# Laying out a small replicated identity matrix on GpSimd instead of VectorE, in a gated scan followed by a soft mixture of experts

## The chip, the core and the metric

The kernel runs on one core of one Trainium2 chip. The core has five engines that each work through their own list of instructions: TensorE (PE in the profile, with PEld for its weight loads), VectorE (DVE), ScalarE (ACT), GpSimd (POOL) and SyncE (SP), which issues the DMA transfers between HBM and the on-chip memory SBUF. TensorE writes its results to a second on-chip memory, PSUM. The engines wait for one another through semaphores. The metric is the device time of one execution in microseconds; a lower time is better.

## The reference

Two layers are computed one after the other. The first is a gated linear recurrence over 5056 time steps, for 4 sequences of 256 channels:

```python
sig_r, sig_i = sigmoid(r_gate), sigmoid(i_gate)
a_t = exp(8 * sig_r * log(sigmoid(a_param)))
x_gated = sqrt(max(1 - a_t * a_t, 1e-6)) * sig_i * x
h = a_t[:, t] * h + x_gated[:, t]          # for each t; y[:, t] = h
```

The second is a soft mixture of 8 experts with 4 slots each, over all 4 x 5056 = 20224 tokens of y (called x below):

```python
logits = x @ phi                                   # 20224 x 32
d = exp(logits - logits.max(0)); d /= d.sum(0) + 1e-9
slot_input = d.T @ x                               # 32 slots x 256
h = maximum(slot_input[e] @ w1[e], 0); slot_out[e] = h @ w2[e]   # each expert e
c = exp(logits - logits.max(1)); c /= c.sum(1) + 1e-9
out = c @ slot_out                                 # 20224 x 256
```

## The kernel before

The 20224 tokens are cut into 40 blocks of up to 512 and 22 units: unit 0 holds one block, units 1 to 18 hold two, the last three hold one. Each unit goes through a fixed set of steps, and a step is a small function that issues one or a few instructions. The names below are those of the order lists.

- `Dr`, `Di`, `Dx` (SP) load the r gate, the i gate and x of a unit.
- `SR`, `SI` (ACT, lines 810 and 828) take the tanh of the gates; `EX` (ACT, 884) makes a_t; `SQ` (mostly POOL, 869) squares it; `RT` (ACT, 900) takes the root of 1 - a_t². ACT works in phases, because tanh and exp on one side and the root on the other need different function tables (ACT_TABLE_LOAD). The roots of three or four units are taken together.
- `U` multiplies the i gate by x for one block, on POOL (850) or, for blocks 2, 8 and a few others, on DVE (848).
- `TU` (PE, 917) transposes a unit's half of U into PSUM; `ST` (DVE, 940) multiplies it by the root; `SC` (DVE, 960) runs the recurrence. In `ST1.0` the first number is the unit and the second the half of the channels.
- `TY` (PE, 983) transposes the result back, `YC` (DVE 999 or ACT 997) copies it from PSUM, `LG` (PE, 1042) makes the logits, `LE` (DVE, 1056) copies them with their running maximum, `TE` (PE, 1066 and 1070) transposes them, `ES` (ACT, 1079) takes the exponentials, `AC` (PE, 1095) sums the slots' inputs.
- Once all units are done, the slots' inputs are merged, the experts run (PE, 1357 and 1409), and for each unit the result is made (PE, 1559), copied (1574, 1576) and stored (SP, 1587).

All data live in one SBUF tensor `all_s` of 49 slots. A planner with a model of durations hands out slots and fixes, for each engine, where TensorE gets filler multiplications of `half_id` (line 1234), which compute nothing that is used. The order of the steps on each engine is written out by hand in the table `ORDER`, one list an engine, and the planner follows it.

The change touches `const` and `const2`. `const` (POOL, lines 692 to 701) builds the 128 x 128 identity `ident`, a bf16 copy `half_id`, its negative `minus`, and a few columns of ones. `const2` (DVE, lines 705 to 709) writes a column `eps` and `R`: 4 x 4 copies of a 32 x 32 identity, which serves as a matrix for sums over groups of partitions. `R` is read for the first time by step `W` (line 1302), after the last scan, and `eps` by the steps `RB` (line 1496), later still. Each of the four copies writes 32 partitions by 128 elements, reading a 32 x 32 piece of `ident` four times over. Before, `const2` stands in the list of DVE between `SC0.1` and `ST1.1`.

Of the kernel before, what the change touches and what calls it, by code (L numbers as in the profile page):

```python
# [11 lines left out]
AF = mybir.ActivationFunctionType  # L12
# [4 lines left out]
J = 4  # L17
# [68 lines left out]
SHIFT = {}  # L86
ORDER = {
    "DVE": (
# [13 lines left out]
    ),  # L102
    "ACT": (
# [27 lines left out]
    ),  # L131
    "POOL": (
# [5 lines left out]
    ),  # L138
# [91 lines left out]
class Planner:  # L230
# [15 lines left out]
    def add(self, eng, name, dur, deps=(), prio=0.0, emit=None, lat=None, alloc=(), uses=(), **kw):  # L246
        eng = eng if isinstance(eng, tuple) else (eng,)
        if lat is None:
            lat = {"PE": 0.25, "ACT": 0.13, "DVE": 0.13, "POOL": 0.12, "SP": 0.05}[eng[0]]
        if eng[0] == "PE":  # L250
            dur *= PEX
        t = Task(eng, name, dur, lat, deps, prio + KOFF.get(re.match("[A-Za-z]+", name)[0], 0.0) + EARLY.get(name, 0.0), emit, alloc, uses, **kw)
        self.tasks.append(t)
        for b in [*alloc, *uses]:
            b.users += 1
        return t
# [308 lines left out]
def kernel(  # L565
# [11 lines left out]
    nc = tc.nc if tc is not None else None  # L577
    B, S, D = x.shape
    E, _, FF = w1.shape
    NS = phi.shape[1]  # L580
# [33 lines left out]
    if tc is not None:  # L614
# [18 lines left out]
        ident = sb.tile([P, P], F32, name="ident")  # L633
# [6 lines left out]
        R = sb.tile([P, J, NS], F32, name="R")  # L640
        ones = sb.tile([1, 1], F32, name="ones")
        eps_sb = sb.tile([P, 1], F32, name="eps")
# [7 lines left out]
    def t(buf):  # L650
        if buf.tag == "s":
            a, n = buf.slot[0], len(buf.slot)
            return all_s[:, a : a + n, :] if n > 1 else all_s[:, a, :]
        if buf.tag == "one" and buf.slot[0] >= len(T["one"]):
            single_banks()
        v = T[buf.tag][buf.slot[0]]
        return v[:, 0, :] if buf.tag == "pair" and buf.tags != ("pair",) else v

    add = planner.add
# [43 lines left out]
    t_const = add("POOL", "const", 0.75, prio=-100, emit=e_const)  # L703

    def e_const2():
        nc.vector.memset(eps_sb, 1e-9)
        for j in range(J):
            v = slice(32 * j, 32 * j + NS)
            nc.vector.tensor_copy(out=R[v], in_=ident[v, v].rearrange("p (o s) -> p o s", o=1).broadcast_to([NS, J, NS]))  # L709

    t_const2 = add("DVE", "const2", 0.9, deps=[t_const], prio=-50, emit=e_const2)


    chunk_of = {}
# [496 lines left out]
    for nm, q in order:  # L1211
        p = q if nm == "r" else unit[q][0]
# [50 lines left out]
    def last_y(pl, tag):  # L1263
# [4 lines left out]
               emit=lambda: nc.gpsimd.memset(t(sT)[:, : E * H * NS], 0.0))  # L1268
# [82 lines left out]
    for e in range(E):  # L1351
# [11 lines left out]
        if not e:  # L1363
# [6 lines left out]
                       prio=-30 + e, emit=e_l1,  # L1370
# [33 lines left out]
    for e in range(E):  # L1404
# [10 lines left out]
        if e == E - 1:  # L1415
            half = [slice(0, P), slice(P, D)]
            l2s = [add("PE", "L2.7", 0.44, deps=[hr[e // EB], wts[("w2", e)][1]], gate=begun(l2_prev),
                       prio=-30 + e + 5.2, emit=lambda f=e_l2: f(cs=half[0]), uses=[wts[("w2", e)][0], hz, so], shape="C")]
# [4 lines left out]
                      prio=-30 + e + 5.2, emit=e_l2, alloc=[] if e else [so],  # L1423
# [4 lines left out]
    def e_rc(v):  # L1428
        if planner.cur.eng_used == "ACT":
            nc.scalar.copy(out=t(soRb)[:, v], in_=t(sr)[:, v])  # L1430
        else:
            nc.vector.tensor_copy(out=t(soRb)[:, v], in_=t(sr)[:, v])

    t_sw = []
    for k, (n_so, n_rs, n_sw) in enumerate((("SO", "RS", "SW"), ("SV", "RV", "SX"))):
        v = half[k]
# [5 lines left out]
                        emit=lambda v=v: e_rc(v), alt={"ACT": 0.21}))  # L1442
# [76 lines left out]
    for i, g in enumerate(corder):  # L1519
# [25 lines left out]
        for p in gunits[g]:  # L1545
# [40 lines left out]
            def e_od(og=og, a0=quads(p0)[0] * QT, c=per_part(p) * (2 if both else 1)):  # L1586
# [4 lines left out]
                deps=group_ev if both else ev, prio=pr + 4, emit=e_od, uses=[og], kind="out", lat=LATO)  # L1591
# [82 lines left out]
```

## Time and profile before

| what | value |
|---|---|
| time, median of 3 runs | 291.35 us (291.05 to 292.14) |
| time of the profiled execution | 290.35 us |
| its span, first to last instruction | 288.6 us |
| mean granted TensorE clock | 0.968 |
| PE busy / DVE busy / ACT busy / POOL busy | 254.1 / 234.2 / 237.1 / 187.0 us |
| HBM read and written | 78.94 MB and 20.71 MB |

The profile records one execution. A busy time is the sum over the span, so it doesn't say where an engine waits. Views used below are the timeline (each row: start, duration, engine, line, operation, output <- inputs, shapes, count, and in brackets the idle time before and what ended it), the chain of work that ended last, and busy time by stretches.

### The profile page before, as it was taken

To read this page: it belongs to the slowest core of one execution; us is meant where nothing else is said; L and a number is where in the kernel's file an instruction comes from. 1 tells how busy PE (TensorE), PEld (TensorE's weight loads), DVE (VectorE), ACT (ScalarE), POOL (GpSimd) and SP (SyncE) were. 2 spreads that over 40 slices of the span, in tenths; PEclk is the share of its full clock that TensorE was granted. 3 is DMA by queue.
4 is the path that set the end of the run, shared out by engine and by line. 5 is a ranking of instruction groups with operands and counts; after the bars stand their busy time and mean duration, and the time that the engine had idled before them with its cause. 6 is when DMAs were issued, how large, how long until landed. Compare 5 with 4: busy or idle time off the path is not lost.

```text
span 288.6 us, 5895 instructions
## 1 busy us (share of the span) xinstructions
PE 254.1 (88%) x2428; PEld 169.4 (59%) x2428; DVE 234.2 (81%) x277; ACT 237.1 (82%) x237; POOL 187.0 (65%) x120
## 2 busy tenths in 40 slices
PE   6999949889999799899899998999999999999800
PEld 2455634665777468568466766666766566656500
DVE  0025999999999999999899999999985579879720
ACT  6999999809999999999999999999980357877500
POOL 2379989399698999998997999996300321222000
PEclk9999986999999999999999999999999999999975
DMA  7999999999966989989999999987770029999995
GB/s 234 412 427 417 420 422 425 417 420 420 408 260 246 420 334 394 417 304 378 340 357 413 419 414 353 400 309 230 250 320 2 2 108 407 417 437 403 429 426 253
DMA packets 14956, 100.02 MB, mean 347 GB/s; under 512 B 1745, under 2 KB 2002, under 8 KB 4306
## 3 DMA queue, kind: packets, MB, share of 16 engines
q1 hardware_dynamic: 14928, 99.65, 85.9%
q8 instruction: 19, 0.31, 0.4%
q14 instruction: 7, 0.06, 0.1%
q10 hardware_dynamic: 2, 0.00, 0.0%
HBM read 78.94 MB, written 20.71 MB: 345 GB/s over the span
## 4 chain that ended last, share of the span: by engine, by line
PE 36%; DVE 25%; ACT 21%; issue 8%; POOL 5%; DMA 1%; DVEq 0%; ACTq 0%; POOLq 0%
DVE all_s L960 11%; PE one L1234 9%; DVE pair L940 7%; PE bank L1559 6%; ACT all_s L884 5%; ACT all_s L900 4%; ACT all_s L828 4%; POOL all_s L869 3%; ACT all_s L810 3%; PE bank L1234 3%; ACT yn L997 3%; PE pair L917 3%; PE bank L1357 2%; PE bank L1409 2%; DVE R L709 2%
## 5 line engine op out<-in xcount | busy, mean ns | idle before, releaser
L960 DVE TENSOR_TENSOR_SCAN all_s<-all_s,pair 128x1024 f32<-128x1024 f32 (+8 forms) x50 | 93.2, 1880 | 0.6
L850 POOL TENSOR_TENSOR all_s<-all_s 128x1024 f32<-128x1024 f32 (+1 forms) x37 | 88.2, 2404 | 5.1 <-ACT all_s L828 3.2
L869 POOL TENSOR_TENSOR all_s<-all_s 128x1024 f32<-128x1024 f32 (+2 forms) x42 | 71.8, 1735 | 22.1 <-ACT all_s L884 15.8
L917 PE MATMUL pair<-ident,all_s 128*128 128x128 f32 x480 | 60.2, 278 | 7.9 <-DVE all_s L960 6.7
L917 PEld LDWEIGHTS pair<-ident,all_s 128*128 128x128 f32 x480 | 53.8, 142 | 16.6 <-DVE all_s L960 7.4
L940 DVE SCALAR_TENSOR_TENSOR pair<-all_s,pair 128x1024 f32<-128x1024 f32 (+1 forms) x38 | 44.7, 1187 | 2.9 <-ACT all_s L900 2.6
L983 PE MATMUL pair<-ident,all_s 128*128 128x128 f32 x316 | 41.5, 277 | 2.5 <-ACT yn L997 1.7
L884 ACT ACTIVATE all_s<-all_s,ca 128x2048 f32<-128x2048 f32 (+3 forms) x28 | 43.4, 1587 | 0.1
L1234 PE MATMUL one<-half_id 128*128 128x512 bf16 x157 | 41.0, 406 | 0.0
L983 PEld LDWEIGHTS pair<-ident,all_s 128*128 128x128 f32 x316 | 34.4, 140 | 11.2 <-ACT yn L997 4.5
L1506 POOL TENSOR_TENSOR all_s<-all_s,rs_all 128x512 f32<-128x512 f32 (+3 forms) x12 | 10.7, 896 | 43.4 <-DVE rs_all L1503 43.4
L1234 PEld LDWEIGHTS <-half_id 128*128 128x128 bf16 x222 | 21.9, 102 | 28.4 <-issue 10.5
L828 ACT ACTIVATE all_s<-all_s 128x2048 f32<-128x2048 f32 (+2 forms) x22 | 37.9, 1730 | 0.0
L810 ACT ACTIVATE all_s<-all_s 128x2048 f32<-128x2048 f32 (+2 forms) x22 | 37.4, 1729 | 0.6 <-DMA all_s<-in_r_gate_dram 0.6
L900 ACT ACTIVATE all_s<-all_s 128x2048 f32<-128x2048 f32 (+2 forms) x22 | 37.1, 1733 | 0.1
L1095 PE MATMUL one<-yn,eS 128*32 128x257 f32 x312 | 22.5, 386 | 2.6 <-ACT eS L1079 1.8
L1574 ACT COPY all_s<-bank 128x512 f32<-128x512 f32 (+1 forms) x37 | 18.8, 551 | 7.2 <-PE bank L1559 5.9
L1042 PE MATMUL one<-all_s,phi_sb 128*32 128x256 f32 (+1 forms) x344 | 23.6, 368 | 0.8 <-DVE all_s L960 0.7
L997 ACT COPY yn<-pair 128x1024 f32<-128x1024 f32 (+1 forms) x24 | 23.2, 987 | 0.0
L1576 DVE COPY all_s<-bank 128x512 f32<-128x512 f32 (+1 forms) x28 | 17.7, 653 | 4.4 <-PE bank L1559 3.2
L999 DVE COPY yn<-pair 128x1024 f32<-128x1024 f32 x16 | 19.3, 1208 | 0.0
L1559 PE MATMUL bank<-all_s,eS 32*128 32x256 f32 x200 | 18.6, 395 | 0.0
(110 smaller groups left out, 302.3 us busy)
## 6 DMA issues: line engine op xcount, KB each, us to landing
all_s<-in_r_gate_dram SPq DMA_DIRECT2D x18, 1024.0 KB, 10.7
all_s<-in_i_gate_dram SPq DMA_DIRECT2D x18, 1024.0 KB, 10.8
all_s<-in_x_dram SPq DMA_DIRECT2D x18, 1024.0 KB, 9.9
all_s<-in_moe_w_dram SPq DMA_DIRECT2D x16, 1024.0 KB, 7.9
out_dram<-all_s SPq DMA_DIRECT2D x5, 2048.0 KB, 9.6
out_dram<-all_s SPq DMA_DIRECT2D x8, 1024.0 KB, 6.5
all_s<-in_i_gate_dram SPq DMA_DIRECT2D x3, 512.0 KB, 8.1
all_s<-in_x_dram SPq DMA_DIRECT2D x3, 512.0 KB, 10.0
```

The lines of the kernel that those rows point to most:

```text
L810: nc.scalar.activation(v, v, AF.Tanh, scale=0.5)
L828: nc.scalar.activation(v, v, AF.Tanh, scale=0.5)
L850: eng.tensor_tensor(out=o, in0=a, in1=b, op=ALU.mult)
L869: eng.tensor_tensor(out=t(Nb[(p, h)])[:, :c], in0=v, in1=v, op=ALU.mult)
L884: nc.scalar.activation(v, v, AF.Exp, scale=ca[:, h : h + 1], bias=ca[:, h : h + 1])
L900: nc.scalar.activation(v, v, AF.Sqrt, bias=f, scale=-f)
L917: nc.tensor.matmul(t(up)[:, i, m * P : (m + 1) * P], raw(nm, q)[:, m * D + h * P : m * D + (h + 1) * P], ident, is_transpose=True, start=( ...
L940: nc.vector.scalar_tensor_tensor(v, w, 1e-3 if gate_of(quads(p)[0]) == "S" else 0.5e-3, u, op0=ALU.max, op1=ALU.mult)
L960: nc.vector.tensor_tensor_scan(dst, dst, flat()[:, s0:s1], init, op0=ALU.mult, op1=ALU.add)
L983: nc.tensor.transpose(out=flat()[:, b * D + h * P : b * D + (h + 1) * P], in_=t(A[p])[:, h, i * QT + (b0 + b) * P : i * QT + (b0 + b + 1) ...
L1234: nc.tensor.matmul(t(b)[:, 0, :] if b.tag == "pair" else t(b), half_id, half_id.rearrange("p (o c) -> p o c", o=1).broadcast_to([P, J, P]) ...
L1559: nc.tensor.matmul(t(op)[:, k * D : (k + 1) * D], t(hT)[r, (k0 + k) * P : (k0 + k + 1) * P], t(soRb)[r, :D], start=True, stop=True)
```

## The change

The step `const2` moves from DVE to POOL, with all of its five instructions, and from its place behind the first scan to the very beginning, directly behind `const`. The planner's estimate of it goes from 0.9 to 1.3 us. In the table, `const2` leaves the DVE list and enters the POOL list; the other lists keep their names and their order.

```diff
     "DVE": (
-        "CA SQ2.1 U2 ST0.0 ST0.1 SC0.0 SC0.1 const2 ST1.1 SC1.1 ST1.0 SC1.0 ST2.0 SC2.0 ST2.1 SC2.1 ST3.0 YC1.0 SC3.0 "
+        "CA SQ2.1 U2 ST0.0 ST0.1 SC0.0 SC0.1 ST1.1 SC1.1 ST1.0 SC1.0 ST2.0 SC2.0 ST2.1 SC2.1 ST3.0 YC1.0 SC3.0 YC3.0 U8 "
...
     "POOL": (
-        "const SQ3.1 SQ3.0 SQ0.1 SQ0.0 U0 SQ1.0 SQ1.1 U1 SQ2.0 U3 P14 U4 U6 U5 SQ5.1 SQ5.0 SQ4.0 SQ4.1 U7 SQ6.1 SQ6.0 "
+        "const const2 SQ3.1 SQ3.0 SQ0.1 SQ0.0 U0 SQ1.0 SQ1.1 U1 SQ2.0 U3 P14 U4 U6 U5 SQ5.1 SQ5.0 SQ4.0 SQ4.1 U7 SQ6.1 "
...
     def e_const2():
-        nc.vector.memset(eps_sb, 1e-9)
+        nc.gpsimd.memset(eps_sb, 1e-9)
         for j in range(J):
             v = slice(32 * j, 32 * j + NS)
-            nc.vector.tensor_copy(out=R[v], in_=ident[v, v].rearrange("p (o s) -> p o s", o=1).broadcast_to([NS, J, NS]))
+            nc.gpsimd.tensor_copy(out=R[v], in_=ident[v, v].rearrange("p (o s) -> p o s", o=1).broadcast_to([NS, J, NS]))
 
-    t_const2 = add("DVE", "const2", 0.9, deps=[t_const], prio=-50, emit=e_const2)
+    t_const2 = add("POOL", "const2", 1.3, deps=[t_const], prio=-50, emit=e_const2)
```

In the built program DVE had these instructions around the place (`SC0.1`, then `const2`, then `ST1.1`, `SC1.1`, `ST1.0`); line numbers are those of the kernel before.

```order
L960 SCALAR_TENSOR_TENSOR all_s<-all_s,pair_74 128x512
L706 MEMSET eps 128x1
L709 COPY R<-ident 32x128 x4
L940 SCALAR_TENSOR_TENSOR pair_75<-all_s,pair_75 128x1024
L960 SCALAR_TENSOR_TENSOR all_s<-all_s,pair_75 128x1024
L940 SCALAR_TENSOR_TENSOR pair_73<-all_s,pair_73 128x1024
```

After the change `ST1.1` stands directly behind `SC0.1`. (Its line numbers are higher by one, since the POOL list takes one more line.)

```order
L961 SCALAR_TENSOR_TENSOR all_s<-all_s,pair_73 128x512
L961 SCALAR_TENSOR_TENSOR all_s<-all_s,pair_74 128x512
L941 SCALAR_TENSOR_TENSOR pair_75<-all_s,pair_75 128x1024
L961 SCALAR_TENSOR_TENSOR all_s<-all_s,pair_75 128x1024
L941 SCALAR_TENSOR_TENSOR pair_73<-all_s,pair_73 128x1024
```

On POOL the end of `const` and the first squares stood like this before the change.

```order
L697 TENSOR_SCALAR minus<-ident 128x128
L699 MEMSET yn_65 128x4
L700 MEMSET ones 1x1
L701 MEMSET one_sb 128x1
L869 TENSOR_TENSOR all_s<-all_s 128x1024 x2
L869 TENSOR_TENSOR all_s<-all_s 128x512 x2
```

After it, the five instructions stand between the last of `const` and the first square.

```order
L701 MEMSET ones 1x1
L702 MEMSET one_sb 128x1
L707 MEMSET eps 128x1
L710 COPY R<-ident 32x128 x4
L870 TENSOR_TENSOR all_s<-all_s 128x1024 x2
L870 TENSOR_TENSOR all_s<-all_s 128x512 x2
```

The lists of ACT and SP hold the same instructions in the same order, and every tile in `all_s` keeps its slot. On PE one filler multiplication is left out: three instead of four stand between `TU2.0` and `TU2.1`.

## Rows read from the trace of the kernel before

**Rows 1.** The chain that ended last, 29 to 41 us: start, us, what

```profile
30.21 1.32 PE pair L917 x12
...
33.03 1.08 DVE R L709
...
38.93 1.24 DVE pair L940
```

**Rows 2.** Timeline of DVE, 25 to 67 us

```profile
28.83 2.33 DVE L960 TENSOR_TENSOR_SCAN all_s<-all_s,pair 128x512 f32<-128x512 f32 x2
31.08 1.94 DVE L709 COPY R<-ident 32x128 f32<-32x128 f32 x1
...
33.03 5.87 DVE L709 COPY R<-ident 32x128 f32<-32x128 f32 x3
...
52.98 1.21 DVE L940 SCALAR_TENSOR_TENSOR pair<-all_s,pair 128x1024 f32<-128x1024 f32 x1
...
58.59 2.83 DVE L848 SCALAR_TENSOR_TENSOR all_s<-all_s 128x1024 f32<-128x1024 f32 x1
```

**Rows 3.** Timeline of POOL, 25 to 67 us

```profile
30.57 2.37 POOL L850 TENSOR_TENSOR all_s<-all_s 128x1024 f32<-128x1024 f32 x1
32.92 1.12 POOL L838 TENSOR_SCALAR all_s<-all_s,one_sb 128x1024 f32<-128x1024 f32 x1
34.12 7.02 POOL L850 TENSOR_TENSOR all_s<-all_s 128x1024 f32<-128x1024 f32 x3
...
56.59 3.75 POOL L869 TENSOR_TENSOR all_s<-all_s 128x1024 f32<-128x1024 f32 x2 [4.64 <-issue]
60.30 3.33 POOL L850 TENSOR_TENSOR all_s<-all_s 128x1024 f32<-128x1024 f32 x1
```

**Rows 4.** Timeline of ACT, 25 to 75 us

```profile
26.54 6.46 ACT L900 ACTIVATE all_s<-all_s 128x1024 f32<-128x1024 f32 x4
...
49.24 4.07 ACT L884 ACTIVATE all_s<-all_s,ca 128x2048 f32<-128x2048 f32 x2
...
64.42 0.49 ACT L1079 ACTIVATE eS<-one 128x384 f32<-128x384 f32 x1 [7.51 <-PE one L1070]
...
66.23 7.31 ACT L900 ACTIVATE all_s<-all_s 128x2048 f32<-128x2048 f32 x4
```

**Rows 5.** Three stretches: PE, PEld, DVE, ACT, POOL busy; clock, DMA, GB/s

```profile
57.00:64.40 7.40, 5.38 (x46) 4.01 (x43) 7.40 (x8) 0.00 (x0) 7.40 (x4) 1.00 1.01 421
64.50:209.00 144.50, 135.81 (x1329) 97.46 (x1327) 141.69 (x123) 144.13 (x118) 128.92 (x71) 1.00 0.90 353
209.00:288.60 79.60, 63.50 (x779) 39.62 (x777) 51.29 (x125) 39.35 (x85) 11.23 (x13) 0.93 0.70 292
```

**Rows 6.** Timeline of the first 13 us, POOL and DVE

```profile
1.37 0.29 POOL L696 CAST half_id<-ident 128x128 bf16<-128x128 f32 x1
1.63 0.53 POOL L697 TENSOR_SCALAR minus<-ident 128x128 f32<-128x128 f32 x1
...
12.06 1.89 POOL L869 TENSOR_TENSOR all_s<-all_s 128x1024 f32<-128x1024 f32 x1 [9.67 <-ACT all_s L884]
...
4.33 0.17 DVE L1146 TENSOR_SCALAR ca<-ca 128x2 f32<-128x2 f32 x1 [4.33 <-ACT ca L1130]
```

**Rows 7.** Timeline of PE, 30 to 50 us

```profile
36.58 1.47 PE L917 MATMUL pair<-ident,all_s 128*128 128x128 f32 x12
...
42.60 2.82 PE L917 MATMUL pair<-ident,all_s 128*128 128x128 f32 x12 [3.68 <-DVE all_s L960]
45.22 3.74 PE L1234 MATMUL one<-half_id 128*128 128x512 bf16 x9
```

**Rows 8.** The load of x for unit 8, and the POOL multiplications that read it

```profile
L748 SPq DMA_DIRECT2D all_s<-in_x_dram x1: 327/327/327, 61.2 to 61.2; - x1
...
DMA to landing us min/median/max: 12.4/12.4/12.4
...
82.25 4.71 POOL L850 TENSOR_TENSOR all_s<-all_s 128x1024 f32<-128x1024 f32 x2 [0.67 <-ACT all_s L828]
```

33 rows, old and new, of the table ORDER are left out of this document.

## The prediction

> **What bounds the kernel now.** I began with the chain that ended last. Around 31 to 39 us it runs through the copies that write `R`, the step that the change moves: the transposes `TU1.1` end at 31.53, then comes `R`, and only at 38.93 the next real work of DVE, `ST1.1` [rows 1]. So the moved step isn't small work hidden somewhere; at this place DVE is what the chain waits for.
>
> The timeline of DVE says how long [rows 2]. Its two scans of unit 0 end at 28.83 + 2.33 = 31.16. The copies begin at 31.08 and the last ends at 33.03 + 5.87 = 38.90. Four copies of 32 x 128 elements thus hold DVE for 7.8 us, while a scan over 128 x 512 takes 1.2. The reader is to compare the ends of the copies with the ends of POOL's instructions [rows 3]: POOL ends one at 30.57 + 2.37 = 32.94, the next at 34.04, and three of 2.34 each at about 36.5, 38.8 and 41.1. The copies end at 33.02, at 34.11 [rows 1] and the last at 38.90, each just behind the end of a POOL instruction. A copy waits for POOL's running instruction and then needs less than 0.1 us.
>
> The timeline of ACT tells whether anybody needs those 7.8 us [rows 4]. ACT idles for 7.51 us before `ES0` at 64.42, so it was free at 56.91; `ES0` waits for `TE0` of PE, which waits for `LE0` of DVE. From there on ACT is the bound: in the 144.5 us from 64.5 to 209 it is busy for 144.13 [rows 5]. DVE is busy for 141.69 there, POOL for 128.92, and the DMA engines at 0.90. The rest, 209 to 288.6, begins when the last scans are through.
>
> So the idle time of ACT is the one large hole in an otherwise closed sequence, about as long as what DVE loses to the copies.
>
> **The change, part by part.**
>
> Removed from DVE: from 31.16, where DVE would be free, to 38.93, where `ST1.1` starts: 7.77 us. The memset of `eps` lies inside.
>
> What is late next: `ST1.1` also needs `TU1.1`, which ends at 31.53 [rows 1], and the third of the four roots. The four end at 26.54 + 6.46 = 33.00 and the large ones take about 1.8 each [rows 4], so the third ends at 31.2. `ST1.1` starts at about 31.55, and 0.39 of the 7.77 goes. That leaves 7.38.
>
> Added to POOL: one memset and four copies, behind `const` at about 2.4 us. The trace has no such copy on POOL. Nearest is the cast of the identity, 128 x 128 with one input, 0.29 us; the bound from above is `minus` at 0.53, from below nothing [rows 6]. I take 0.29, since it too is a copy of the same length along the partition: 4 x 0.29 + 0.1 = 1.3 us, so POOL ends at 3.7. The cover is POOL's idle time of 9.67 us up to 12.06 [rows 6]; without it the 1.3 us would lie on POOL's squares. The next DVE instructions, which make `ca`, start at 4.33, behind that end. Cost 0.
>
> PE has one filler less between `TU2.0` and `TU2.1`: about 0.2 us, where PE waited 3.68 us before [rows 7]. Worth nothing by itself.
>
> Is DVE then held elsewhere? From 38.93 to 52.98 there are four pairs of a multiplication and a scan, 3.51 each [rows 1, 2]. `ST2.0` would start at 31.55 + 7.03 = 38.6; its transposes `TU2.0` end at 36.58 + 1.47 = 38.05, whatever DVE does [rows 7]. Half a microsecond of room. `ST3.0` would start at 45.6. Its transposes stand on PE behind three fillers, `TU2.1`, nine fillers and the logits of unit 2. Four fillers took from 38.05 to 38.92 (42.60 less the wait of 3.68), 0.22 each; the nine took 3.74, or 0.42 each, behind the long wait, where the twelve transposes also took 2.82 instead of 1.47 [rows 7]. By 0.22 the nine end at 42.2, just when unit 2's scan ends, and the logits (some 0.6) and sixteen transposes (2.0) at 44.8: in time. By 0.42 it is 46.5, and 0.9 us is lost. I take 0, because the wait that went ahead of the slow pace is gone, and keep 0.9 for the range.
>
> `U8`, on DVE with two inputs in SBUF, took 2.83 us while POOL was at work; a multiplication of the same shape with one input in PSUM takes 1.21 [rows 2]. It moves to 51.2. POOL has a hole there, from 51.95 (56.59 less 4.64) [rows 3]; `U8` ends by 53.2 instead of 54.0, another 0 to 0.9 us. I count none of it, since the next term caps the gain.
>
> `ES0` comes at 64.42 - 7.38 = 57.04, with ACT free at 56.91. ACT's hole shrinks to 0.1, and its whole closed block moves forward by 7.4. More than 7.51 isn't to be had here.
>
> Can the others follow? POOL: the fourth root of the second group starts at about 66.23 + 3 x 1.8 = 71.7, after the change at 64.3, and needs the squares of unit 7 [rows 4]. POOL waited 4.64 us before the squares of unit 6; they need the exponentials that end at 49.24 + 4.07 = 53.31. From 53.4: two squares 3.75, one multiplication 2.37 to 3.33, two squares 3.75, so 63.3 to 64.2 [rows 3, 4]. It just fits. The loads: DMA is full from 57 to 64.4 (1.01, 421 GB/s) [rows 5], so these can't come sooner. The tightest that I found is x of unit 8, issued at 61.2 and landed 12.4 later, at 73.6; it is used at 82.25, then at 74.9 [rows 8]. It fits by 1.3. Later, DMA has a tenth to spare and the issues move with the slots that come free.
>
> Sum: -7.77 + 0.39 + 0 + 0 = -7.4 us. The profiled execution goes from 290.35 (span 288.6 and 1.75 around it) to 283.0. The median of the runs stands 1.0 higher, and I carry the difference over: 291.35 - 7.4 = **284.0**.
>
> **A rule to weigh.** The rows show copies that end 0.1 us behind POOL's instructions, and pairs of `ST` and `SC` that keep 3.51 us throughout. The Trainium skill, SBUF — State Buffer, section "SBUF: two separate sides", says that VectorE and GpSimd share a pair of ports as an exclusive lock, which a VectorE instruction takes in a two-port mode or with two SBUF inputs, and that the loser blocks for the other's whole instruction. The trace agrees in the copies (7.8 us for four). It speaks against the change in one respect: copies on GpSimd could hold the lock against the instructions that make `ca`. By the rule with 0.29 each the lock is free at 3.7 and the sum stays -7.4.
>
> **The rivals.**
> - *POOL doesn't follow.* The profile names nothing that ended POOL's wait of 4.64 us. If the squares of unit 6 can't start before 56.59, those of unit 7 end where they did, about 67.4, instead of 64.3 when ACT wants them: 3.1 lost, 291.35 - 4.3 = 287.1. For it: the wait is unexplained and POOL's fit is within 0.1 to 1. Against: it is more likely a wait for a slot that PE and DVE free, which moves too. A load tighter than the one I found, or slow fillers (284.9), lie in the same region.
> - *The wait only finds another victim.* DVE's next instructions would wait for POOL's in the place of the copies: 291.3. For: POOL works without a break from 30.57 to 41.1 [rows 3]. Against: two scans ran in 2.33, and the pairs took 3.51 beside a busy POOL [rows 2].
> - *Slower.* GpSimd could be very slow at reading a 32-element piece four times over; no row shows it. The squares at 12.06 would then be late, and `U0` and the first scans behind them. This decides from an end at 12.06 + 7.4 = 19.5, that is over 4.2 us a copy; at 5 us, POOL ends at 22.5 and the time is 291.35 - 7.4 + 10.4 = 294.4. Against: 0.29 to 0.53 for 128 partitions.
>
> **How the numbers follow.** Full gain 70% (283.0 to 284.9), part of it 18% (284.9 to 288), the other victim 8% (290 to 291.8), slower 4%. The likeliest gives 284.0. Dropping the last two cases and the upper end of the second, the range is 282.9 to 287.2; its lower end allows for 1 us from a shorter `U8` and from the spread of the runs (1.1). Under 0.5% (1.5 us) this kernel's measurement can't tell a change from none. Faster by more: 70 + 18 and a little of the third, 89%. Same: 7%. Slower: 4%.
>
> **What would show it.** `ST1.1` at about 31.6; no copy of `R` on DVE; five POOL instructions that end before 4.3; ACT's idle time before `ES0` under 1 us; the squares of unit 6 at 53 to 54; ACT still without a gap until about 201; the last span about 281. I am wrong if DVE's next instructions stretch, if ACT's hole comes back in front of a root or a tanh, or if loads end a wait of ACT or POOL after 57 us.

## The result and the profile after

| | before | after |
|---|---|---|
| median of the runs shown together | 291.06 us (289.14 to 292.14, 6 runs) | 283.38 us (282.77 to 283.72, 6 runs) |
| profiled execution | 290.35 us | 283.55 us |
| its span | 288.6 us | 281.8 us |
| DVE busy / ACT busy | 234.2 / 237.1 us | 225.7 / 237.0 us |

The ratio is 0.9736, with an interval of 0.9703 to 0.9768: 7.7 us less by the medians, where 7.4 were forecast. The kernel before spreads by 3 us from run to run (289.14 to 292.14), and beside e9 to e12 below the same two kernels took 289.22 and 282.9 us, 6.3 apart. So the size of the gain is known only to about a microsecond.

The timelines of the changed kernel answer to those of before. First POOL in its first 13 us, for [rows 6]:

```profile
2.31 0.09 POOL L707 MEMSET eps<- 128x1 f32 x1
2.34 1.27 POOL L710 COPY R<-ident 32x128 f32<-32x128 f32 x4
```

The four copies take 1.27 us together and end at 3.61, before DVE's next work on `ca` at 3.87. Then DVE from 25 to 67 us, for [rows 2]:

```profile
29.55 2.32 DVE L961 TENSOR_TENSOR_SCAN all_s<-all_s,pair 128x512 f32<-128x512 f32 x2
32.11 1.23 DVE L941 SCALAR_TENSOR_TENSOR pair<-all_s,pair 128x1024 f32<-128x1024 f32 x1 [0.23 <-PE pair L918]
...
51.77 1.99 DVE L849 SCALAR_TENSOR_TENSOR all_s<-all_s 128x1024 f32<-128x1024 f32 x1
...
54.82 0.54 DVE L1057 TENSOR_SCALAR_CACHE_REDUCE all_s<-one 128x384 f32<-128x384 f32 x1
```

`ST1.1` follows the scans after 0.23 us, in which DVE waits for the transposes. `U8` (line 849) takes 1.99 us, where it took 2.83. ACT in the same time, for [rows 4]:

```profile
27.25 6.47 ACT L901 ACTIVATE all_s<-all_s 128x1024 f32<-128x1024 f32 x4
...
53.95 3.71 ACT L829 ACTIVATE all_s<-all_s 128x2048 f32<-128x2048 f32 x2
57.56 0.47 ACT L1080 ACTIVATE eS<-one 128x384 f32<-128x384 f32 x1
...
59.34 7.31 ACT L901 ACTIVATE all_s<-all_s 128x2048 f32<-128x2048 f32 x4
```

The row of `ES0` has no bracket any more: the hole of 7.51 us is gone, and ACT goes from one tanh to `ES0` without a stop. POOL, for [rows 3]:

```profile
31.29 2.38 POOL L851 TENSOR_TENSOR all_s<-all_s 128x1024 f32<-128x1024 f32 x1
...
50.30 2.38 POOL L851 TENSOR_TENSOR all_s<-all_s 128x1024 f32<-128x1024 f32 x1
54.12 3.75 POOL L870 TENSOR_TENSOR all_s<-all_s 128x1024 f32<-128x1024 f32 x2 [1.44 <-ACT all_s L885]
57.83 2.39 POOL L851 TENSOR_TENSOR all_s<-all_s 128x1024 f32<-128x1024 f32 x1
60.17 3.75 POOL L870 TENSOR_TENSOR all_s<-all_s 128x1024 f32<-128x1024 f32 x2
```

POOL waited 4.64 us before the squares of unit 6; now it waits 1.44, and what ends the wait is named: the exponentials of ACT. PE, for [rows 7]:

```profile
37.06 1.47 PE L918 MATMUL pair<-ident,all_s 128*128 128x128 f32 x12
38.37 0.81 PE L1235 MATMUL one<-half_id 128*128 128x512 bf16 x3
39.02 1.47 PE L918 MATMUL pair<-ident,all_s 128*128 128x128 f32 x12
40.33 2.11 PE L1235 MATMUL one<-half_id 128*128 128x512 bf16 x9
```

The second twelve transposes take 1.47 us instead of 2.82, and the nine fillers 2.11 instead of 3.74. Busy time by stretches, for [rows 5]; the last two are the stretches behind `ES0` and behind the last scans:

```profile
49.60:57.00 7.40, 6.21 (x53) 4.38 (x53) 7.40 (x8) 7.40 (x5) 5.96 (x4) 1.00 1.01 422
57.00:201.60 144.60, 135.21 (x1323) 96.73 (x1322) 141.03 (x122) 144.24 (x117) 132.83 (x73) 1.00 0.94 374
201.60:281.80 80.20, 63.98 (x783) 40.11 (x781) 51.75 (x126) 39.83 (x87) 11.23 (x13) 0.93 0.71 292
```

Ahead of the second stretch ACT is now busy for 7.40 of 7.40 us, where it did nothing for as long. Behind it the time is the same, though POOL and the loads are a little busier there (132.83 against 128.92 us, 374 against 353 GB/s). From `ES0` to the end of the span there are 288.6 - 64.42 = 224.2 us before and 281.8 - 57.56 = 224.2 after, and the four roots that started at 66.23 [rows 4] start at 59.34, 6.9 earlier. The whole gain lies ahead of `ES0`.

The chain that ended last says the same. Before, it went through `R` on DVE [rows 1]; after, in 25 to 66 us, it is on ACT once `U2` on DVE is through:

```profile
24.57 2.69 DVE all_s L849
...
27.25 6.47 ACT all_s L901 x4
...
57.66 0.37 ACT eS L1080
...
59.34 7.31 ACT all_s L901 x4
```

One difference between the two profiled executions isn't the change. In the one after, the third load of the r gate ended a longer wait of ACT at the start:

```profile
9.50 1.91 ACT L811 ACTIVATE all_s<-all_s 128x2048 f32<-128x2048 f32 x1 [1.75 <-DMA all_s<-in_r_gate_dram]
```

Before, that row began at 8.79, behind 0.57 us. All that ACT does from there on is 0.71 us late, up to the first roots (27.25 against 26.54 [rows 4]). The kernel of before with one tanh left out (e8 below) has this wait too, at 1.69 us, and over all of the traces below it lies between 0.91 and 1.99, whatever the kernel. So it varies from execution to execution, and the profiled pair shows -7.5 + 0.7 = -6.8 us. The medians show -7.7, which is 0.2 more than the hole held and within the spread of the runs.

### The profile page after: what moved, and what is told of

The parts are those of the page before. It is cut to its first block, busy times and chain, and to the rows that moved or that the text cites. A ratio compares the mean times of both kernels' runs of the same rounds, so it can differ in the third digit from the quotient of the medians.

```text
span 281.8 us, 5894 instructions
## 1 busy us (share of the span) xinstructions
PE 251.6 (89%) x2427; PEld 167.7 (60%) x2427; DVE 225.7 (80%) x272; ACT 237.0 (84%) x237; POOL 187.0 (66%) x125
## 4 chain that ended last, share of the span: by engine, by line
ACT 41%; PE 26%; DVE 8%; issue 8%; DMA 6%; POOL 4%; SPq 2%; DVEq 0%; ACTq 0%
ACT all_s L885 10%; ACT all_s L901 8%; ACT all_s L811 8%; ACT all_s L829 7%; DMA all_s<-in_x_dram 6%; PE bank L1560 6%; DVE all_s L961 4%; PE bank L1235 3%; ACT yn L998 3%; PE bank L1358 3%; PE bank L1410 3%; DVE pair L941 2%; POOL all_s L870 2%; PE pair L918 2%; POOL all_s L851 2%
## 5 line engine op out<-in xcount | busy, mean ns | idle before, releaser
L851 POOL TENSOR_TENSOR all_s<-all_s 128x1024 f32<-128x1024 f32 (+1 forms) x37 | 87.0, 2371 | 1.6 <-DMA all_s<-in_x_dram 1.2
L918 PE MATMUL pair<-ident,all_s 128*128 128x128 f32 x480 | 58.9, 275 | 4.5 <-DVE all_s L961 3.0
L918 PEld LDWEIGHTS pair<-ident,all_s 128*128 128x128 f32 x480 | 52.7, 140 | 13.2 <-issue 5.7
L984 PE MATMUL pair<-ident,all_s 128*128 128x128 f32 x316 | 41.5, 277 | 2.6 <-ACT yn L998 1.7
L984 PEld LDWEIGHTS pair<-ident,all_s 128*128 128x128 f32 x316 | 34.4, 140 | 11.2 <-ACT yn L998 4.5
L1235 PE MATMUL one<-half_id 128*128 128x512 bf16 x156 | 39.6, 397 | 0.0
```

The lines of the kernel that those rows point to most:

```text
L851: eng.tensor_tensor(out=o, in0=a, in1=b, op=ALU.mult)
L918: nc.tensor.matmul(t(up)[:, i, m * P : (m + 1) * P], raw(nm, q)[:, m * D + h * P : m * D + (h + 1) * P], ident, is_transpose=True, start=( ...
L984: nc.tensor.transpose(out=flat()[:, b * D + h * P : b * D + (h + 1) * P], in_=t(A[p])[:, h, i * QT + (b0 + b) * P : i * QT + (b0 + b + 1) ...
L1235: nc.tensor.matmul(t(b)[:, 0, :] if b.tag == "pair" else t(b), half_id, half_id.rearrange("p (o c) -> p o c", o=1).broadcast_to([P, J, P]) ...
```

## The experiments

Theory: the copies were dear because each waited for the GpSimd instruction that was running, and they stood on the path to `ES0`, the one hole of ACT. Any place or form without that wait is worth the same, up to the point where ACT has no hole left. The rivals: it is GpSimd's speed or the early place that matters; it is the mere occupation of DVE; or ACT isn't what sets the pace afterwards. All ratios are to the kernel before on the same chip, which took 289.88 us beside e1 to e4, 290.39 beside e5 to e8 and 289.22 beside e9 to e12. The changed kernel itself ran beside e9 to e12 only, with a ratio of 0.979 (e11).

**e1: on DVE, but at the beginning.** The table of DVE, against the kernel before:

```diff
-        "CA SQ2.1 U2 ST0.0 ST0.1 SC0.0 SC0.1 const2 ST1.1 ...
+        "CA const2 SQ2.1 U2 ST0.0 ST0.1 SC0.0 SC0.1 ST1.1 ...
```

> The step stays on VectorE and moves alone, to directly behind the two instructions that make ca, at about 4.4 us, when GpSimd is idle. My theory (the four copies are short and only wait for GpSimd's running instructions): each copy takes at most 0.15 us there, and the time is that of the changed kernel, 283.4 us within 0.7. Rival (the copies are slow on VectorE by themselves, 1.9 us each): four copies of about 1.9 us in the rows, still hidden ahead of 19 us, so the time would be 283.4 too and the rows decide. Rival (the engine is what counts, not the place): about 291.

Measured: 283.46 us, ratio 0.9789 (0.9743 to 0.9835). In the timeline of DVE:

```profile
4.56 0.21 DVE L709 COPY R<-ident 32x128 f32<-32x128 f32 x1
...
4.78 0.68 DVE L709 COPY R<-ident 32x128 f32<-32x128 f32 x3
```

DVE needs 0.22 us a copy when POOL is idle, more than the 0.15 expected, against 1.95 at the old place. The ratio is that of e11, so GpSimd itself isn't needed for the gain.

**e2: on POOL, but in the middle.** The table of POOL, against the changed kernel:

```diff
-        "const const2 SQ3.1 SQ3.0 SQ0.1 SQ0.0 U0 SQ1.0 SQ1.1 U1 SQ2.0 U3 P14 U4 ...
+        "const SQ3.1 SQ3.0 SQ0.1 SQ0.0 U0 SQ1.0 SQ1.1 U1 SQ2.0 U3 const2 P14 U4 ...
```

> The step goes to GpSimd, but to the place in GpSimd's list that runs at about 33 us, between U3 and P14, where it ran on VectorE before. My theory: the copies take about 0.3 us each, 1.3 in all; U4 and the transposes behind it come 1.3 late, the second multiplication of VectorE 0.9 late, of which 0.8 is room ahead of ES0; 283.4 to 284.2 us. Rival (GpSimd is as tight as ScalarE there, all 1.3 us count): 284.7. Rival (only leaving GpSimd's busy stretch helps): near 291.

Measured: 283.03 us, ratio 0.977 (0.9722 to 0.9817). The timeline of POOL:

```profile
33.42 1.27 POOL L710 COPY R<-ident 32x128 f32<-32x128 f32 x4
34.79 1.12 POOL L839 TENSOR_SCALAR all_s<-all_s,one_sb 128x1024 f32<-128x1024 f32 x1
35.99 7.02 POOL L851 TENSOR_TENSOR all_s<-all_s 128x1024 f32<-128x1024 f32 x3
42.97 3.75 POOL L870 TENSOR_TENSOR all_s<-all_s 128x1024 f32<-128x1024 f32 x2
```

In the middle of POOL's other work, with DVE busy too, the copies take their 1.27 us, as at the start. What they delay is taken up where POOL had 0.9 us of idle time before the squares at 42.97, which now follow at once. The early place isn't needed either.

**e3: the old place on DVE, in another form.** A reduction over one element writes the same numbers:

```diff
-            nc.vector.tensor_copy(out=R[v], in_=ident[v, v].rearrange("p (o s) -> p o s", o=1).broadcast_to([NS, J, NS]))
+            nc.vector.tensor_reduce(out=R[v], in_=ident[v, v].rearrange("p (o s u) -> p o s u", o=1, u=1).broadcast_to([NS, J, NS, 1]), axis=AX.X, op=ALU.max)
```

> VectorE, the old place, the old sizes; only the operation differs: a maximum over one element (a reduction) in place of a copy. My theory (the wait belongs to the form of the instruction, which wants what GpSimd holds): if a reduction doesn't want it, four of at most 0.3 us, ST1.1 about 0.9 us later than in the changed kernel, of which 0.8 is room: 283.4 to 284.2 us. Rival (any VectorE instruction that reads and writes SBUF waits for GpSimd at this place): four of about 1.9 us and 291 us.

Measured: 283.31 us, ratio 0.978 (0.9731 to 0.9829). The timelines of POOL and of DVE at the place:

```profile
31.42 2.38 POOL L850 TENSOR_TENSOR all_s<-all_s 128x1024 f32<-128x1024 f32 x1
33.78 1.13 POOL L838 TENSOR_SCALAR all_s<-all_s,one_sb 128x1024 f32<-128x1024 f32 x1
...
31.93 0.27 DVE L709 TENSOR_REDUCE R<-ident 32x128 f32<-32x128 f32 x1
...
32.22 0.86 DVE L709 TENSOR_REDUCE R<-ident 32x128 f32<-32x128 f32 x3
33.11 1.23 DVE L940 SCALAR_TENSOR_TENSOR pair<-all_s,pair 128x1024 f32<-128x1024 f32 x1
```

One POOL instruction runs from 31.42 to 33.80, and the four reductions run right through it, 0.28 us each. Same engine, same place, same bytes: 7.8 us as copies, 1.2 as reductions. Alone, the four copies take 0.9 us (e1), so 6.9 of the 7.8 us at the old place were the wait for POOL, and the wait comes with the form of the instruction: the copy has it, the reduction hasn't. The remaining 1.2 us of DVE cost nothing that the runs can tell. The Trainium skill, SBUF — State Buffer, section "SBUF: two separate sides", ties the wait to a two-port mode or to two inputs in SBUF. By the Trainium skill, VectorE: DVE Perf Modes, section "The perf-mode tier table (the rule you actually need)", a reduction has only the plain mode. The trace agrees, with 0.28 against 1.95 us beside a busy POOL.

**e4: on DVE, late.** `const2` stands in DVE's table between `MX` and `AE10`, shortly before `R` is first read:

```diff
-        "... RR3 AE9 MX AE10 W AE11 ...
+        "... RR3 AE9 MX const2 AE10 W AE11 ...
```

> VectorE, but late: between MX and AE10, after the last scan, where GpSimd is idle and VectorE waited 0.47 us. My theory: four copies of about 0.1 us, inside that wait, 283.4 us within 0.7. Rival (slow on VectorE by themselves): four of 1.9 us on the path to the experts, 283.4 + 7.3 = 290.7.

Measured: 283.47 us, ratio 0.9785 (0.9734 to 0.9836), with 0.21 us for the first copy at 205.84 and 0.68 for the other three. The place costs nothing once POOL has little to do.

**e5 and e6: one or three copies stay on DVE at the old place**, the others are made by POOL at the beginning. Against the changed kernel, for e5 (3 in the place of 1 for e6):

```diff
-        for j in range(J):
+        for j in range(1, J):
...
+    def e_const3():
+        for j in range(1):
+            v = slice(32 * j, 32 * j + NS)
+            nc.vector.tensor_copy(out=R[v], in_=ident[v, v].rearrange("p (o s) -> p o s", o=1).broadcast_to([NS, J, NS]))
...
-        "CA SQ2.1 U2 ST0.0 ST0.1 SC0.0 SC0.1 ST1.1 ...
+        "CA SQ2.1 U2 ST0.0 ST0.1 SC0.0 SC0.1 const3 ST1.1 ...
```

> As the changed kernel, but one of the four copies of R stays on VectorE at the old place. My theory (a copy costs what is left of GpSimd's running instruction, and ScalarE's hole ahead of ES0 leaves VectorE 0.8 us of room): GpSimd's U3 ends at about 33.7, ST1.1 starts 1.6 us later than in the changed kernel, ScalarE idles 0.8 us ahead of ES0, 284.2 us (283.8 to 284.8). Rival (every copy costs a quarter of the whole gain): 283.4 + 1.9 = 285.3.

> As the changed kernel, but three of the four copies stay on VectorE at the old place. My theory: the third ends with GpSimd's U4 at about 37.3, ST1.1 starts 5.2 us later, 0.8 of it is room, ScalarE idles about 4.4 us ahead of ES0 and the time is 287.8 us (287.2 to 288.5). Rival (a quarter each): 283.4 + 5.8 = 289.2. Rival (the gain is lost as soon as any copy waits): 291 for this and for one copy alike.

Measured: e5 283.14 us, ratio 0.9762 (0.9729 to 0.9795); e6 288.74 us, ratio 0.9954 (0.9917 to 0.9991). DVE's timeline of e5:

```profile
32.03 1.96 DVE L717 COPY R<-ident 32x128 f32<-32x128 f32 x1
33.92 1.21 DVE L948 SCALAR_TENSOR_TENSOR pair<-all_s,pair 128x1024 f32<-128x1024 f32 x1
...
53.56 1.22 DVE L856 SCALAR_TENSOR_TENSOR all_s<-all_s 128x1024 f32<-128x1024 f32 x1
...
55.82 0.55 DVE L1064 TENSOR_SCALAR_CACHE_REDUCE all_s<-one 128x384 f32<-128x384 f32 x1
```

The one copy costs 1.96 us and `ST1.1` starts 1.8 later than in the changed kernel, and yet no time is lost; the expectation of 284.2 (283.8 to 284.8), with room for 0.8 us, missed. Three terms add up. `U8` takes 1.22 instead of 1.99 us, since POOL is idle when it comes, and so `LE0` (line 1064) starts 1.0 late instead of 1.8; the expectation lacked this term. `LE0` stood 2.74 us ahead of `ES0` in the changed kernel (54.82 to 57.56), while in e6, where ACT waits for it, 1.95 are enough: the 0.8 us of room. And all of this execution, ACT too, is 0.25 late from the load at the start (its row begins at 9.75, not 9.50). So `LE0` stands 1.98 ahead of `ES0` at 57.80: just enough, and one copy used up the room. The rows of e6 for POOL, DVE and ACT:

```profile
31.24 2.38 POOL L858 TENSOR_TENSOR all_s<-all_s 128x1024 f32<-128x1024 f32 x1
33.59 1.13 POOL L846 TENSOR_SCALAR all_s<-all_s,one_sb 128x1024 f32<-128x1024 f32 x1
34.81 7.03 POOL L858 TENSOR_TENSOR all_s<-all_s 128x1024 f32<-128x1024 f32 x3
...
54.95 3.75 POOL L877 TENSOR_TENSOR all_s<-all_s 128x1024 f32<-128x1024 f32 x2 [2.32 <-ACT all_s L892]
...
31.74 5.51 DVE L717 COPY R<-ident 32x128 f32<-32x128 f32 x3
37.28 1.23 DVE L948 SCALAR_TENSOR_TENSOR pair<-all_s,pair 128x1024 f32<-128x1024 f32 x1
...
56.95 2.83 DVE L856 SCALAR_TENSOR_TENSOR all_s<-all_s 128x1024 f32<-128x1024 f32 x1
...
60.83 0.54 DVE L1064 TENSOR_SCALAR_CACHE_REDUCE all_s<-one 128x384 f32<-128x384 f32 x1
...
62.78 0.49 ACT L1087 ACTIVATE eS<-one 128x384 f32<-128x384 f32 x1 [5.18 <-PE one L1078]
```

With three copies `ST1.1` is 37.28 - 32.11 = 5.17 later than in the changed kernel; less the 0.8 of slack, and with `U8` back at 2.83 (0.84 more), the hole should be 5.2, and is 5.18. The expectation of 287.8 (287.2 to 288.5) missed on the other side, since it took the hole at 4.4, without `U8`. The profiled execution took 288.87 us, 5.3 more than that of the changed kernel. Beyond the 0.8 us of room, a microsecond on DVE here is a microsecond of the kernel.

**e7 and e8: ACT one tanh lighter**, behind the hole in the changed kernel (unit 7), ahead of it in the kernel before (unit 6, with `p == 6`):

```diff
         def e_si():
+            if p == 7:
+                return
```

> The changed kernel without the tanh of the i gate of unit 7, an instruction of 1.9 us on ScalarE behind ES0 (the i gate enters U untouched there, so the output differs). My theory (behind the change ScalarE alone sets the pace up to 200 us): 1.8 us less, 281.6 us, or somewhat more where GpSimd or VectorE, which have 12 and 3 us of idle time in that stretch, take over; 281.4 to 282.6. Rival (the loads or VectorE set the pace): no change, 283.4.

> The kernel before the change without the tanh of the i gate of unit 6, an instruction of 1.9 us on ScalarE just ahead of the hole in front of ES0 (the i gate enters U untouched there, so the output differs). My theory (VectorE sets the time of ES0, ScalarE waits for it): the hole grows from 7.5 to 9.3 us and the time stays, within 0.5%. Rival (ScalarE's work counts everywhere): 1.8 us less than before.

Measured: e7 282.75 us, ratio 0.9742 (0.9706 to 0.9778); e8 290.75 us, ratio 1.0016 (0.999 to 1.0041). e8 came out as the theory says: ACT's hole only grows.

```profile
65.12 0.49 ACT L1081 ACTIVATE eS<-one 128x384 f32<-128x384 f32 x1 [9.33 <-PE one L1072]
```

e7 gave less than the expected 1.8 us and lies just above its range. Its timeline of ACT has two waits that the changed kernel hasn't:

```profile
67.80 3.72 ACT L811 ACTIVATE all_s<-all_s 128x2048 f32<-128x2048 f32 x2 [0.43 <-DMA all_s<-in_r_gate_dram]
...
77.72 3.71 ACT L811 ACTIVATE all_s<-all_s 128x2048 f32<-128x2048 f32 x2 [0.43 <-DMA all_s<-in_r_gate_dram]
```

So the loads stand close behind ACT after the change. Four more runs beside one another follow that up.

**e9 and e10: seven eighths of one load left out**, unit 7's i gate, in e9 without that unit's tanh too, in e10 with it. **e11** is the changed kernel and **e12** is e7, beside them. The edit of e9 and e10:

```diff
-                nc.sync.dma_start(out=t(b), in_=rows.rearrange("p (i f) -> p i f", i=2))
+                part = 1024 // 8 if (nm, p) == ("i", 7) else 1024
+                nc.sync.dma_start(out=t(b)[:, :, :part], in_=rows.rearrange("p (i f) -> p i f", i=2)[:, :, :part])
```

> The changed kernel without the tanh of unit 7's i gate, and with only one eighth of the columns of that gate loaded (the rest keeps what the slot held before). Dropping the tanh alone gave 0.6 us by the medians (282.75), because ACT then waited twice, 0.43 us each, for loads of r behind unit 7. Theory (the load stream, full at 1.01 from 57 us on, is the next bound, 2.48 us a load): the loads behind come 2.2 us sooner, ACT waits for none of them, and the whole 1.8 us of the tanh comes out: 281.6 (281.0 to 282.0). Rival (something other than loads took the gain): as without the tanh alone, 282.75, and ACT waits elsewhere between 60 and 90 us.

> The changed kernel with only one eighth of the columns of unit 7's i gate loaded, all of ACT's work left in place. Theory (after the change ACT's work sets the pace, the loads only stand close behind): no gain, 283.4 within 0.5 us, and ACT without a wait from 57 to 200 us as before. Rival (the load stream already sets the pace): up to 2.2 us less, 281.2 to 282.5.

> The changed kernel itself, beside the three others: 283.4 (282.8 to 283.7), as the measure for them.

> The changed kernel without the tanh of unit 7's i gate once more, beside the others. Theory (part of the 1.8 us goes to waits for loads, and how much depends on when the load stream starts in each execution): between 281.6 and 283.0, over 0.4 us less than the changed kernel beside it, and ACT waits for loads of r around 67 and 77 us. Rival (the earlier value was chance): 283.4, no difference.

Measured, with the ratio to the kernel before:

| kernel | us | ratio |
|---|---|---|
| e11, the changed kernel | 282.9 | 0.979 (0.9757 to 0.9822) |
| e10, one load less | 283.29 | 0.9799 (0.9767 to 0.9831) |
| e12, one tanh less | 282.21 | 0.977 (0.974 to 0.9801) |
| e9, both less | 282.05 | 0.9761 (0.9731 to 0.9791) |

The intervals of these ratios overlap, so the medians alone tell little (e12 lies 0.7 us under e11, e9 0.85); the traces tell more. e10: the load alone gives nothing, and from 57 to 205 us the waits list none of ACT for a load. e12 waits for the same two loads as e7, 0.48 and 0.45 us. In e9 both of these waits are gone, as the theory says, but the full 1.8 us didn't come: two other waits of ACT stand later, both for PE.

```profile
102.61 1.01 ACT L1001 COPY yn<-pair 128x1024 f32<-128x1024 f32 x1 [0.19 <-PE pair L987]
...
107.42 0.60 ACT L1083 ACTIVATE eS<-one 128x512 f32<-128x512 f32 x1 [0.19 <-PE one L1074]
```

These two waits hold 0.4 us of the 0.7 that is missing; where the other 0.3 went, the views don't show. From `ES0` to the end of the span it is 224.2 us in the changed kernel, 223.3 in e7 (280.3 - 56.98), 223.5 in e12 (280.3 - 56.75) and 223.1 in e9 (280.1 - 57.04). In e10 and e11, where nothing shortens ACT's work, it is 224.1 and 224.3. Of a tanh of 1.8 us, 0.7 to 0.9 comes out as long as the loads stand, and 1.1 without them; single traces of equal work differ by 0.2, so what the load adds is small and barely shown. My expectation of e9, 281.6, was too hopeful by half a microsecond, and its rival wrong about the waits. After the change ACT leads, but of a microsecond saved there the loads and PE take back a part.

## Why the prediction was right

Forecast 284.0 us in a range of 282.9 to 287.2, measured 283.38. By its steps:

- *Removed.* `ST1.1` was to start 0.39 us behind the end of the scans; it starts 0.23 behind it. e3 shows the reason itself: without the wait for POOL, the same writes at the same place cost no time. That a copy itself needs less than 0.1 us was misread: alone it takes 0.22 (e1). No term of the sum used it.
- *Added to POOL.* Four copies at 0.29, done by 3.7; measured 281 to 292 ns each in e2, and 3.61 for the end. The rival of a slow GpSimd falls with this.
- *Is DVE held elsewhere?* The nine fillers took 2.11 us at 0.23 each, so the 0.22 that I took was right and the 0.9 us of the range wasn't needed.
- *`U8`.* Shorter by 0.84, inside the 0 to 0.9 that I didn't count. It made the slack of 0.8 us before `ES0` that e5 used up. Nothing of it reached the time, since ACT was no longer waiting.
- *`ES0` and the cap.* The hole was to shrink from 7.51 to 0.1 and is 0. ACT's whole block moved by 6.9 us between the two profiled executions, or 7.6 without the 0.7 of the late load at the start.
- *POOL follows.* The squares of unit 6 were to start at 53.4; they start at 54.12, 53.4 plus that 0.7, and end their wait on the exponentials. The pairs of squares and the multiplication between them end at 60.17 + 3.75 = 63.9, or 63.2 without the 0.7: the early end of the forecast 63.3 to 64.2. That rival falls. What POOL had waited for, which the profile didn't name, can be read from three traces: the squares start 0.13 or 0.14 us behind the end of PE's transposes of a result (line 983 in the kernel before) in the kernel before (56.46, 56.59), in e6 (54.81, 54.95) and in e8 (57.15, 57.29). These transposes wait for a copy of DVE. So the wait did move with DVE, as I had argued, until the exponentials came last; in e6 these had ended at 54.00, so they aren't what its row should name.
- *The wait finds another victim.* None did: the pairs of DVE keep their pace, and DVE's busy time fell by 8.5 us, 7.8 for the copies and 0.8 for `U8`.
- *The loads.* I wrote that a load ending a wait of ACT or POOL after 57 us would show me wrong. One does: POOL waits 1.17 us for x at 146.81. It delays nothing, for ACT has no wait for POOL or a load from 57 to 205 us, only 0.7 us for PE. The sign was too strict. The room of x of unit 8 came out as forecast: issued at 54.49, it landed 19.8 later, at 74.3, and the sixth of the seven multiplications that run from 63.88 for 16.37 us reads it at about 75.6, so 1.3 are left. But the loads that e7 and e12 ran into, with one tanh less, were two of r, which I hadn't sized.
- *From the profile to the median.* I carried over that the median stood 1.0 above the profiled execution. It doesn't any more: the profiled execution was to take 283.0 and took 283.55 with the late load's 0.7 in it, and the median is 283.38, 0.2 below it. So the two deviations partly cancel, and that 284.0 came within 0.6 us is in part luck.

What no run settles is why `U8` finds POOL where it does in a given execution; I only read it from the rows.

## What to carry to other kernels

A small instruction's price on VectorE can lie wholly in what GpSimd is doing at that moment: compare the ends of the two engines' rows, and if they coincide, move it to where GpSimd is idle, or change its form; which engine did it mattered little here (e1, e2). Then look for who waits at the end of the path: the gain is capped by the idle time of the next engine, here ACT's one hole of 7.5 us. Once such a hole is closed, another engine may stand close behind: here about half of the next 1.8 us saved on ACT was lost again to waits for loads and TensorE.

## What the runs showed of the hardware

The ends of DVE's copies fit those of POOL's instructions to a few hundredths. In e6 POOL's instructions end at 33.62, 34.72 and 37.17 us and the copies of DVE at 33.70, 34.80 and 37.25: 0.08 behind each. `U8`, with two inputs in SBUF, ends 1.07 or 1.08 us behind the POOL instruction that it meets in twelve of the fourteen traces, among them before (61.42, where the squares end at 60.34), after (53.76, 52.68) and e6 (59.78, 58.70). It took 2.83, 1.99 and 2.83 us there, and 1.22 in e5, where POOL is idle when it starts. It works the other way too: in e5 POOL's next two squares begin while `U8` still runs and take 4.02 us instead of 3.75.

I hadn't seen that DVE's wait also cost TensorE its clock. Busy time by stretches of the kernel before:

```profile
39.00:42.50 3.50, 0.00 (x0) 0.00 (x0) 3.46 (x3) 3.47 (x3) 2.61 (x2) 0.88 1.01 419
42.50:45.30 2.80, 2.70 (x13) 2.64 (x14) 2.77 (x3) 2.80 (x2) 2.71 (x2) 0.50 1.02 424
45.30:49.00 3.70, 3.65 (x10) 1.12 (x8) 3.66 (x3) 3.70 (x3) 3.70 (x3) 0.57 1.01 421
```

PE was idle for 3.68 us while DVE made `R`, and the granted clock behind it was 0.50, the lower level of 1.2 GHz. That is why twelve transposes took 2.82 instead of 1.47 us [rows 7], and nine fillers 3.74. In the changed kernel the same three stretches have 1.00. It cost nothing in time, for DVE, not PE, was late there: its pairs keep 3.51 us in both kernels. But it was the reason for the 0.9 us in my range, and the granted clock of that stretch names it.
